# Keys and queries of six batches: transposed by DMA from a cast DRAM scratch instead of by TensorE

## The chip, the cores and the metric

One core of one Trainium2 chip. The metric is the device time of one execution in microseconds (us). All runs told of here are in the fast state, but for one of the 21 runs of the kernel before on the chip of e8, e10 and e11, which is slow and left out of the ratios. PE is TensorE, DVE is VectorE, ACT is ScalarE, POOL is GpSimd, SP is SyncE. SBUF and PSUM are the two memories on the chip that the kernel works in; PE's results land in PSUM.

## The reference

Attention with a window of 32 to each side and 8 global tokens, then a two-layer MLP on its output. Cut to what matters:

```python
# q, k, v: (8 batches, 8 heads, 576 tokens, 64), float32
scores = q @ k^T / 8
mask   = |i - j| <= 32  or i is global  or j is global
attn   = softmax(where(mask, scores, -1e9))
x      = (attn @ v) as (8*576 tokens, 512)
h      = x @ w_in                    # 512 -> 2048
out    = (relu(h) ** 2) @ w_out      # 2048 -> 512, float32
```

## The kernel before

A *pair* is two heads of one batch: 4 pairs per batch, 32 in all, each worked in two halves of 288 queries (*half-steps*). Attention needs keys and queries with the head dimension on the partitions. So each pair is loaded as float32 with tokens on the partitions, cast to float16 by DVE (keys, `natk`) and ACT (queries, values), transposed by six PE instructions per tensor into a PSUM buffer `tr`, and copied from there by DVE into `kt` and `qt`:

```python
def cast_tokens(op, nm, i):
    b, hp = divmod(i, NHP)
    n = TP + NG if b > 1 else TP           # 96 token rows, 8 global rows
    nat = nats[(nm, i)] = sbt("nat" + nm, [TP + NG, TJ, P], FP16, bufs=2)
    op(out=nat[0:n].rearrange("p j (h d) -> p h j d", d=D),
       in_=st[nm][0:n, 2 * hp : 2 * hp + 2])

def transposed(nm, i):
    nat = nats.pop((nm, i))
    b = i // NHP
    tr = pst("mm" if b == 0 or (nm == "q" and i <= 2 * NHP) else "tr", [P, 1024], FP16)
    for j in range(TJ):                    # 6
        n = TP + NG if (b > 1 and j == TJ - 1) else TP
        nc.tensor.transpose(tr[:, TP * j : TP * j + n], nat[0:n, j, :], identity[0:n, 0:n])
    # ... batches 0 and 1: global rows by 6 small matmuls more
    return tr[:, 0:S].rearrange("p (j q) -> p q j", j=TJ), gl

def tr_k(i, tail=None):                    # tr_q alike, with two copies
    tk, gl = transposed("k", i)
    # ... three DVE copies from PSUM into kts[i % NBUF]
```

The blocks of the MLP of earlier tokens fill PE while attention waits for ACT and DVE. `fill` issues such blocks up to a credit, and `scatter` lets POOL write a finished batch's global rows into `xT`, the input of the MLP. The loop over batches 2 to 7:

```python
for i in range(2 * NHP, B * NHP):
    b, hp = divmod(i, NHP)
    # ...
    for half in range(2):
        et = scores(i, half)
        if i + 1 < B * NHP:
            (tr_k, tr_q)[half](i + 1)
        nf = 3.2 if b == 2 else 4
        fill(2 * step, nf)
        if prev is not None:
            pv(*prev)
            if prev[1] == 1 and prev[0] % NHP == NHP - 1:
                scatter(prev[0] // NHP)
        fill(2 * step + 1, nf)
        prev = (i, half, et)
        casts(i + 2, half)                 # cast_tokens, cast_values, next loads
        step += 1
```

The softmax here doesn't subtract the row's maximum and nothing guards it: scores larger than these inputs give would overflow.

## Time and profile before

| | before |
|---|---|
| time | 369.43 us, median of the first 3 runs (368.81 to 369.75) |
| PE busy, of a span of 368.4 us | 347.7 us (94%) |
| DVE / ACT / POOL busy | 250.5 (68%) / 249.2 (68%) / 51.3 us (14%) |
| DMA packets | 65,011 |

The averages mix stages. I divide the span at the first score matmul of pair 8 (start of batch 2), at that of pair 12 (start of batch 3), and 1.0 us before the end of the last attention matmuls (at 302.45 us here, at 291.41 us in the changed kernel); what follows is MLP, but for these. In the table of windows each row has the stretch and its length, the busy us and the instruction count of PE, its weight loads, DVE, ACT and POOL, then the granted PE clock (1.00 is full speed), the DMA share (how much of the 16 DMA engines' time the recorded packets fill) and GB/s. Batch 2 and batches 3 to 7 of the kernel before:

```profile
80.01:116.46 36.45, 32.35 (x270) 16.36 (x270) 26.92 (x67) 29.61 (x58) 6.84 (x14) 0.95 0.66 166
116.46:301.45 184.99, 182.74 (x1509) 95.63 (x1508) 152.33 (x380) 151.88 (x299) 16.98 (x46) 1.00 0.39 105
```

PE is 99% busy in the second row. In the first it idles for 4.1 us (36.45 - 32.35). These two stages are the ones that the change touches.

### The profile page before, as it was taken

To read this page: it belongs to the slowest core of one execution; us is meant where nothing else is said; L and a number is where in the kernel's file an instruction comes from. 1 tells how busy PE (TensorE), PEld (TensorE's weight loads), DVE (VectorE), ACT (ScalarE), POOL (GpSimd) and SP (SyncE) were. 2 spreads that over 40 slices of the span, in tenths; PEclk is the share of its full clock that TensorE was granted. 3 is DMA by queue.
4 is the path that set the end of the run, shared out by engine and by line. 5 is a ranking of instruction groups with operands and counts; after the bars stand their busy time and mean duration, and the time that the engine had idled before them with its cause. 6 is when DMAs were issued, how large, how long until landed. Compare 5 with 4: busy or idle time off the path is not lost.

```text
span 368.4 us, 8258 instructions
## 1 busy us (share of the span) xinstructions
PE 347.7 (94%) x2941; PEld 186.0 (51%) x2941; DVE 250.5 (68%) x656; ACT 249.2 (68%) x482; POOL 51.3 (14%) x143
## 2 busy tenths in 40 slices
PE   7779799988899999999999999999999989999995
PEld 3556575544445555555555555555555544444442
DVE  7753566656888878977897789778977953422421
ACT  6656574465997799679967996799679942612610
POOL 5364430016000610020002000200020001000000
PEclk9978999998999999999999999999999999999999
DMA  8999999787843663375336533652020011002002
GB/s 196 192 147 201 193 228 201 188 188 193 188 130 97 188 166 94 90 188 142 95 93 187 142 95 93 187 140 60 30 87 2 0 52 64 0 30 85 0 32 85
DMA packets 65011, 43.93 MB, mean 119 GB/s; under 512 B 42730, under 2 KB 60074, under 8 KB 64970
## 3 DMA queue, kind: packets, MB, share of 16 engines
q1 hardware_dynamic: 59752, 38.03, 40.0%
q0 software_dynamic: 4800, 4.79, 7.9%
q10 hardware_dynamic: 418, 0.59, 0.7%
q8 instruction: 23, 0.38, 0.5%
q14 instruction: 18, 0.15, 0.1%
HBM read 37.85 MB, written 9.73 MB: 129 GB/s over the span
## 4 chain that ended last, share of the span: by engine, by line
PE 60%; issue 14%; DVE 7%; DMA 6%; ACT 5%; POOL 4%; POOLq 2%; ACTq 0%; SPq 0%; DVEq 0%
PE mm L502 25%; PE mm L460 24%; PE acc L602 4%; PE tr L415 3%; DMA w_in<-in_moe_w_in_dram 3%; PE sc L564 3%; DVE gt L466 2%; DMA stq<-in_q_dram 2%; POOLq L649 2%; ACT rl L465 2%; DMA stv<-in_v_dram 1%; POOL xT L658 1%; ACT er L570 1%; ACT natq L386 1%; DVE et L574 1%
## 5 line engine op out<-in xcount | busy, mean ns | idle before, releaser
L502 PE MATMUL mm<-w_out,gt 128*128 128x512 f16 x576 | 133.6, 379 | 0.0
L460 PE MATMUL mm<-xT,w_in 128*128 128x512 f16 x512 | 120.7, 382 | 1.0 <-POOL xT L658 1.0
L465 ACT ACTIVATE rl<-mm 128x512 f16<-128x512 f32 x128 | 72.2, 595 | 34.6 <-PE mm L460 33.9
L502 PEld LDWEIGHTS <-gt 128*128 128x128 f16 x576 | 53.1, 97 | 55.6
L460 PEld LDWEIGHTS <-w_in 128*128 128x128 f16 x512 | 47.7, 98 | 51.2 <-issue 2.9
L612 ACT ACTIVATE rec<-acc 64x288 f32<-64x288 f32 (+1 forms) x112 | 45.5, 406 | 33.9 <-PE acc L602 24.1
L638 DVE TENSOR_TENSOR xT<-acc,rec 64x288 f16<-64x288 f32 (+1 forms) x112 | 50.9, 454 | 19.8 <-ACT rec L613 18.0
L466 DVE TENSOR_TENSOR gt<-rl 128x512 f16<-128x512 f16 x128 | 50.2, 421 | 18.2 <-ACT rl L465 17.5
L658 POOL COPY xT<-gx 128x4 f16 (+2 forms) x80 | 21.8, 272 | 231.1 <-DVE xT L638 226.8
L570 ACT ACTIVATE er<-sc 128x912 f16<-128x912 f32 (+1 forms) x48 | 44.0, 917 | 5.4 <-PE sc L564 5.0
L574 DVE TENSOR_TENSOR et<-er,mask 128x912 f16<-128x912 f16 (+1 forms) x48 | 29.9, 623 | 21.2 <-ACT er L570 20.9
L508 DVE COPY ot<-mm 128x512 f32<-128x512 f32 x36 | 24.9, 691 | 26.0 <-PE mm L502 25.3
L613 ACT ACTIVATE rec<-rec 128x288 f32<-128x288 f32 x64 | 28.3, 443 | 2.0
L386 ACT CAST natq<-stq 104x768 f16<-104x768 f32 (+1 forms) x32 | 26.4, 824 | 4.4 <-DMA stq<-in_q_dram 4.4
L570 ACT ACTIVATE et<-sc 128x912 f16<-128x912 f32 (+1 forms) x16 | 14.6, 915 | 12.0 <-PE sc L564 11.7
L386 DVE CAST natk<-stk 104x768 f16<-104x768 f32 (+1 forms) x32 | 17.7, 552 | 0.3
L479 PE MATMUL mm<-xT,w_in 128*128 128x256 f16 x128 | 16.8, 290 | 0.6 <-POOL xT L658 0.6
L479 PEld LDWEIGHTS <-w_in 128*128 128x128 f16 x128 | 12.7, 104 | 3.3 <-issue 0.6
L617 DVE TENSOR_REDUCE gs<-acc 128x16 f32<-128x32 f32 x32 | 6.0, 187 | 12.2 <-ACT rec L612 12.2
L415 PE MATMUL tr<-identity,natk 96*128 96x96 f16 x168 | 12.1, 208 | 1.9 <-DVE natk L386 1.8
L415 PEld LDWEIGHTS <-natq 96*128 96x128 f16 x192 | 9.2, 98 | 7.1 <-ACT natq L386 1.5
L491 DVE TENSOR_TENSOR gt<-rl 128x512 f16<-128x512 f16 x16 | 6.8, 426 | 8.4 <-ACT rl L490 8.1
(205 smaller groups left out, 324.2 us busy)
## 6 DMA issues: line engine op xcount, KB each, us to landing
stk<-in_k_dram SPq DMA_DIRECT2D x32, 288.0 KB
out_dram<-ot SPq DMA_DIRECT2D x36, 256.0 KB
stq<-in_q_dram SPq DMA_DIRECT2D x30, 288.0 KB
stv<-in_v_dram SPq DMA_DIRECT2D x64, 120.0 KB
w_in<-in_moe_w_in_dram POOLq DMA_DIRECT2D x4, 512.0 KB, 9.5
w_out<-in_moe_w_out_dram POOLq DMA_DIRECT2D x4, 512.0 KB, 9.0
stv<-in_v_dram SPq DMA_DIRECT2D x32, 48.0 KB
stq<-in_q_dram ACTq DMA_DIRECT2D x2, 288.0 KB
```

What stands on the lines that cost most here:

```text
L386: op(out=nat[0:n].rearrange("p j (h d) -> p h j d", d=D), in_=st[nm][0:n, 2 * hp : 2 * hp + 2],)
L415: nc.tensor.transpose(tr[:, TP * j : TP * j + n], nat[0:n, j, :], identity[0:n, 0:n])
L460: nc.tensor.matmul(ph, w_in[:, t, u * P : (u + 1) * P], xT[:, t, XOFF + c * TC : XOFF + (c + 1) * TC], start=(t == 0), stop=(t == NDM - 1),)
L465: nc.scalar.activation(out=rl, in_=ph, func=AF.Relu)
L466: nc.vector.tensor_tensor(out=gts[c][:, u, :], in0=rl, in1=rl, op=ALU.mult)
L479: nc.tensor.matmul(ph[:, j], w_in[:, t, (u + j) * P : (u + j + 1) * P], xT[:, t, half * (256 + XOFF) : half * (256 + XOFF) + 256], start=( ...
L502: nc.tensor.matmul(po, gts[c][:, f, m * P : (m + 1) * P], w_out[:, f, :], start=(f == 0), stop=(f == NFF - 1),)
L570: nc.scalar.activation(out=er[:, :, 0:W], in_=sc[:, :, 0:W], func=AF.Exp, bias=0.0, scale=scale)
L574: nc.vector.tensor_tensor(out=et[:, :, 0:W], in0=er[:, :, 0:W], in1=mask[:, MB[half] : MB[half] + W].unsqueeze(1).to_broadcast((P, 2, W)), ...
L612: nc.scalar.activation(out=rec[r], in_=av[rs, xs, :, 0:GTOK], func=AF.Ln)
L613: nc.scalar.activation(out=rec, in_=rec, func=AF.Exp, scale=-1.0)
L638: nc.vector.tensor_tensor(out=xT[r, hp, x0 : x0 + HS].rearrange("p (k x) -> p k x", k=2), in0=av[r, x, :, 0:GTOK], in1=rec[r], op=ALU.mult,)
```

## The change

The intent: for batches 2 to 7, take the transposes off PE and the casts and PSUM copies off DVE and ACT, and let the DMA engines do both. DMAs from POOL cast keys and queries of a whole batch, nine in all, from the float32 inputs into a float16 scratch in DRAM. A transposing DMA from SP brings each pair's 128 columns from there into `kt` or `qt`. Values are cast by their own DMA, straight into place. From batch 3 on they lie in the old float32 buffers of keys and queries (`vbs`), which need constant ones between the values and some zeros; `open_values` writes these once for each of the two buffers.

```diff
+    def fetch_batch(b, nms="kq"):           # POOL: cast on the way to the scratch
+        if "k" in nms:
+            for t in range(NT):
+                r0 = t * P + NG
+                nc.gpsimd.dma_start(
+                    out=kscr[b][r0 : r0 + KN[t]].rearrange("s (h d) -> s h d", d=D),
+                    in_=k[b, :, KT * t : KT * t + KN[t]].rearrange("h s d -> s h d"),
+                )
+        # ... "q" alike, four groups into qscr[b]
+    def fetch_transposed(i):                # SP
+        b, hp = divmod(i, NHP)
+        cols = slice(P * hp, P * hp + P)
+        nc.sync.dma_start_transpose(out=kts[i % NBUF], in_=kscr[b][:, cols])
+        nc.sync.dma_start_transpose(out=qts[i % NBUF], in_=qscr[b][:, cols])
+    def open_values(op, vb):
+        op(vb[:, :, :, 1], 1.0)
+        op(vb[96:P, 4, :, 0], 0.0)
     # ... batch 1: the casts of batch 2 are issued after the transposes of pair 5, and in pair 7:
-            (tr_k, tr_q)[half](i + 1)
+            if more:
+                (tr_k, tr_q)[half](i + 1)     # ... v_globals as before
+            else:
+                fetch_transposed(2 * NHP + half)
     # ... the loop over batches 2 to 7:
-            if i + 1 < B * NHP:
-                (tr_k, tr_q)[half](i + 1)
+            if half and i + 2 < B * NHP:
+                fetch_transposed(i + 2)
             nf = 3.2 if b == 2 else 4
             # ... fill, pv, scatter, fill as before
-            casts(i + 2, half)
+            if half and b + 1 < B and hp < 3:
+                if hp == 0:
+                    open_batch(b + 1)
+                    fetch_batch_globals(b + 1)
+                if hp < 2:
+                    fetch_batch(b + 1, "kq"[hp])
+                else:
+                    fetch_batch_values(b + 1)
+            if half == 0 and b == 2 and hp < 2:
+                open_values(nc.vector.memset, vbs[1 - hp])
```

More of the change, by code (lines that the diff above doesn't have):

```diff
@@ L78, in pst @@
         return ps.tile(shape, dtype, name=tag, tag=tag, bufs=bufs_of[tag])
-    st = {nm: sbt("st" + nm, [TP + NG, H, TJ, D], FP32) for nm in "kq"}
+    stf = {nm: sbt("st" + nm, [P, H * TJ * D], FP32) for nm in "kq"}
+    st = {nm: t[0:TP].rearrange("p (h j d) -> p h j d", j=TJ, d=D) for nm, t in stf.items()}
+    vbs = [
+        stf[nm].bitcast(FP16)[:, 0 : NT * H * P].rearrange("p (t h x d) -> p t h x d", t=NT, x=2, d=D)
+        for nm in "qk"
+    ]
     st["v"] = sbt("stv", [P, NT, H, D], FP32)
@@ L117, in fetch_values @@
         )
-    def fetch_globals(b, hp):
-        def rows(nm):
-            return gscr[(nm, b // 2)][b % 2, :, 2 * hp : 2 * hp + 2]
-        for nm in "kq":
-            js = range(TJ) if b == 2 else (TJ - 1,)
-            for h in range(2):
-                dst = st[nm][TP : TP + NG, 2 * hp + h, js[0] : TJ]
-                nc.sync.dma_start(
-                    out=dst, in_=rows(nm)[:, h].unsqueeze(1).to_broadcast((NG, len(js), D))
-                )
-        nc.sync.dma_start(
-            out=st["v"][0:NG, :, 2 * hp : 2 * hp + 2].rearrange("p t h d -> p t (h d)"),
-            in_=rows("v").rearrange("g h d -> g (h d)").unsqueeze(1).to_broadcast((NG, NT, 2 * D)),
+    kscr, qscr = {}, {}
@@ new lines, in open_batch @@
+    def open_batch(b):
+        kscr[b] = dram.tile([NT * P, dm], FP16, name=f"kscr{b}")
+        qscr[b] = dram.tile([NCOL, dm], FP16, name=f"qscr{b}")
+        pad = 8 + KN[4]
+        nc.sync.dma_start(out=kscr[b][4 * P + pad : NT * P], in_=idle[0 : P - pad, 0:dm])
+    def fetch_batch(b, nms="kq"):
[5 more added lines that the diff above has]
+                    in_=k[b, :, KT * t : KT * t + KN[t]].rearrange("h s d -> s h d"),
+                )
+        if "q" in nms:
+            for g in range(4):
+                r0 = g * GRP
+                nc.gpsimd.dma_start(
+                    out=qscr[b][r0 : r0 + GTOK].rearrange("s (h d) -> s h d", d=D),
+                    in_=q[b, :, GTOK * g : GTOK * (g + 1)].rearrange("h s d -> s h d"),
+                )
@@ new lines, in fetch_batch_globals @@
+    def fetch_batch_globals(b):
+        for nm, scr, r0, n, m in (("k", kscr, 0, NT, P), ("q", qscr, GTOK, 4, GRP)):
+            rows = gscr[(nm, b // 2)][b % 2].rearrange("g h d -> g (h d)")
+            nc.sync.dma_start(
+                out=scr[b].rearrange("(t r) c -> r t c", r=m)[r0 : r0 + NG],
+                in_=rows.unsqueeze(1).to_broadcast((NG, n, dm)),
+            )
+    def fetch_transposed(i):
[3 more added lines that the diff above has]
+        nc.sync.dma_start_transpose(out=qts[i % NBUF], in_=qscr[b][:, cols])
@@ new lines, in open_values, with fetch_batch_values, fetch_values16 @@
+    def open_values(op, vb):
+        op(vb[:, :, :, 1], 1.0)
+        op(vb[96:P, 4, :, 0], 0.0)
+    def fetch_batch_values(b):
+        vb = vbs[b % 2]
+        for t in range(NT):
+            nc.gpsimd.dma_start(
+                out=vb[8 : 8 + KN[t], t, :, 0],
+                in_=v[b, :, KT * t : KT * t + KN[t]].rearrange("h s d -> s h d"),
+            )
+            nc.sync.dma_start(out=vb[0:NG, t, :, 0], in_=gscr[("v", b // 2)][b % 2])
+    def fetch_values16(i):
+        b, hp = divmod(i, NHP)
+        vt = vts[i % NBUF]
+        for e in range(2):
+            nc.gpsimd.dma_start(
+                out=vt[8 : 8 + KT, 0:4, 2 * e],
+                in_=v[b, 2 * hp + e, 0 : 4 * KT].rearrange("(t s) d -> s t d", s=KT),
+            )
+            nc.sync.dma_start(
+                out=vt[0:NG, :, 2 * e],
+                in_=gscr[("v", b // 2)][b % 2, :, 2 * hp + e].unsqueeze(1).to_broadcast((NG, NT, D)),
+            )
+        nc.gpsimd.dma_start(
+            out=vt[8 : 8 + KN[4], 4, 0:3:2],
+            in_=v[b, 2 * hp : 2 * hp + 2, 4 * KT : S].rearrange("h s d -> s h d"),
@@ L362, in gather_rows @@
     def gather_rows(c):
-        gsts = {nm: sbt("gst" + nm, [P, D], FP32) for nm in "kqv"}
+        gsts = {nm: sbt("gst" + nm, [P, D], FP16) for nm in "kqv"}
         for nm, gst in gsts.items():
@@ L373, in gather_store @@
         for nm, gst in gsts.items():
-            scr = dram.tile([P, D], FP32, name=f"gscr_{nm}{c}")
+            scr = dram.tile([P, D], FP16, name=f"gscr_{nm}{c}")
             nc.gpsimd.dma_start(out=scr, in_=gst)
@@ L382, in cast_tokens @@
     def cast_tokens(op, nm, i):
-        b, hp = divmod(i, NHP)
-        n = TP + NG if b > 1 else TP
-        nat = nats[(nm, i)] = sbt("nat" + nm, [TP + NG, TJ, P], FP16, bufs=2)
-        op(
-            out=nat[0:n].rearrange("p j (h d) -> p h j d", d=D),
-            in_=st[nm][0:n, 2 * hp : 2 * hp + 2],
+        hp = i % NHP
+        nat = nats[(nm, i)] = sbt("nat" + nm, [TP, TJ, P], FP16, bufs=2)
+        op(
+            out=nat.rearrange("p j (h d) -> p h j d", d=D),
+            in_=st[nm][:, 2 * hp : 2 * hp + 2],
         )
@@ L410, in transposed @@
         nat = nats.pop((nm, i))
-        b = i // NHP
-        tr = pst("mm" if b == 0 or (nm == "q" and i <= 2 * NHP) else "tr", [P, 1024], FP16)
+        tr = pst("mm" if i < NHP or (nm == "q" and i <= 2 * NHP) else "tr", [P, 1024], FP16)
         for j in range(TJ):
-            n = TP + NG if (b > 1 and j == TJ - 1) else TP
             nc.tensor.transpose(
-                tr[:, TP * j : TP * j + n], nat[0:n, j, :], identity[0:n, 0:n]
+                tr[:, TP * j : TP * j + TP], nat[:, j, :], identity[0:TP, 0:TP]
             )
-        gl = tr[:, S : S + NG]
-        if b < 2:
-            gl = tr.bitcast(FP32)[:, 384 : 384 + NG]
-            for j in range(TJ):
-                nc.tensor.matmul(
-                    gl, nat[0:TP, j, :], ohp[0:TP, j, :], start=(j == 0), stop=(j == TJ - 1),
-                    skip_group_check=True,
-                )
+        gl = tr.bitcast(FP32)[:, 384 : 384 + NG]
+        for j in range(TJ):
+            nc.tensor.matmul(
+                gl, nat[:, j, :], ohp[0:TP, j, :], start=(j == 0), stop=(j == TJ - 1),
+                skip_group_check=True,
+            )
         return tr[:, 0:S].rearrange("p (j q) -> p q j", j=TJ), gl
@@ L582, in pv @@
         b, hp = divmod(i, NHP)
-        vt = vts[i % NBUF]
-        vtf = vt.rearrange("p t x d -> p t (x d)")
+        if b < 3:
+            vt = vts[i % NBUF]
+            vtf = vt.rearrange("p t x d -> p t (x d)")
+            off = (0, D)
+        else:
+            vtf = vbs[b % 2].rearrange("p t h x d -> p t (h x d)")
+            off = (2 * P * hp, 2 * P * hp + D)
         acc = pst("acc", [P, 2, 512])
@@ L602, in pv @@
                 nc.tensor.matmul(
-                    acc[:, e, o : o + w], vtf[:, t, D * e : D * e + P], et[:, e, so : so + w],
+                    acc[:, e, o : o + w], vtf[:, t, off[e] : off[e] + P], et[:, e, so : so + w],
                     start=(n == 0), stop=(n == nw - 1), skip_group_check=True,
@@ L745, in casts @@
             cast_values(op_v, i)
-            if i + NHP < B * NHP:
-                fetch_pair(*divmod(i + NHP, NHP))
-                fetch_globals(*divmod(i + NHP, NHP))
     nc.sync.dma_start(out=gate[:, 0:2], in_=w_in[0:1, 0, dff - 514 : dff - 512])
@@ L777 @@
     gather_store(1, gs1)
+    open_batch(2)
+    fetch_batch_globals(2)
     casts(NHP, 0)
@@ L802 @@
     prev = None
+    pool.tensor_copy(out=gate[:, 0:1], in_=st["k"][32:33, H - 1, TJ - 1, D - 1 : D])
+    fetch_batch(2)
+    fetch_values16(2 * NHP)
+    fetch_values16(2 * NHP + 1)
     for i in range(NHP + 1, 2 * NHP):
-        casts(i + 1, 0)
-        casts(i + 1, 1, nc.vector.tensor_copy)
+        more = i + 1 < 2 * NHP
+        if more:
+            casts(i + 1, 0)
+            casts(i + 1, 1, nc.vector.tensor_copy)
         for half in range(2):
@@ L809 @@
                 pv(*prev)
-            (tr_k, tr_q)[half](i + 1)
-            if half and i + 1 < 2 * NHP:
-                v_globals(i + 1)
+            if more:
+                (tr_k, tr_q)[half](i + 1)
+                if half:
+                    v_globals(i + 1)
+            else:
+                fetch_transposed(2 * NHP + half)
             take(2)
             prev = (i, half, et)
+    fetch_values16(2 * NHP + 2)
     pv(*prev)
     scatter(1)
+    fetch_values16(2 * NHP + 3)
     step = 16
     prev = None
-    casts(2 * NHP + 1, 0)
-    casts(2 * NHP + 1, 1)
     for i in range(2 * NHP, B * NHP):
@@ L837 @@
             prev = (i, half, et)
-            casts(i + 2, half)
+            if half and b + 1 < B and hp < 3:
[4 more added lines that the diff above has]
+                    fetch_batch(b + 1, "kq"[hp])
+                else:
+                    fetch_batch_values(b + 1)
+            if half == 0 and b == 2 and hp < 2:
+                open_values(nc.vector.memset, vbs[1 - hp])
             step += 1
```

## The prediction

> **What bounds the kernel now.** I read the busy time of each engine stage by stage first, because the change touches batches 2 to 7 only and the averages of the whole span (PE 94%) mix stages. The stage borders come from the score matmuls (line 564): pair 8, the first of batch 2, has its first one at 80.0 us and its second half at 87.7; pair 12, the first of batch 3, starts at 116.5; the last attention work ends near 302. In the table of windows the columns are busy us and instruction count per engine, then granted clock, DMA share and GB/s:
>
> ```profile
> 78.00:87.70 9.70, 7.16 (x49) 3.00 (x49) 5.25 (x14) 4.16 (x9) 4.66 (x11) 0.82 0.86 193
> 91.40:100.10 8.70, 7.55 (x71) 4.04 (x70) 6.97 (x18) 8.56 (x18) 0.00 (x0) 1.00 0.89 214
> 100.10:109.10 9.00, 8.53 (x74) 4.38 (x76) 7.76 (x21) 8.86 (x19) 0.00 (x0) 1.00 0.45 113
> ...
> 186.14:223.03 36.89, 36.62 (x304) 19.24 (x305) 30.56 (x77) 30.56 (x61) 2.47 (x8) 1.00 0.47 127
> 223.03:259.92 36.89, 36.62 (x305) 19.24 (x305) 30.57 (x77) 30.58 (x61) 2.47 (x8) 1.00 0.41 109
> ```
>
> From 116 us on PE is busy 36.62 of every 36.89 us, at full clock: it sets the pace. DVE and ACT are busy 83% each and run beside it. Only batch 2 is mixed: ACT fills 8.56 of 8.70 and 8.86 of 9.00 us there, and PE idles about 1.6 us.
>
> Busy PE is not PE at its peak, so I then read the timeline of PE in steady state (start, duration, engine, line, operation, count):
>
> ```profile
> 199.91 0.43 PE L415 MATMUL tr<-identity,natk 96*128 96x96 f16 x6
> 200.18 1.89 PE L460 MATMUL mm<-xT,w_in 128*128 128x512 f16 x8
> 201.91 0.55 PE L602 MATMUL acc<-et,vt_78 128*128 128x112 f16 x6
> 202.29 1.89 PE L460 MATMUL mm<-xT,w_in 128*128 128x512 f16 x8
> 204.11 0.36 PE L564 MATMUL sc<-qt_74,kt_69 64*128 64x112 f16 x6
> 204.41 0.43 PE L415 MATMUL tr<-identity,natq 96*128 96x96 f16 x6
> 204.68 1.89 PE L460 MATMUL mm<-xT,w_in 128*128 128x512 f16 x8
> ```
>
> Starts, not durations, tell the cost. Eight MLP matmuls take 201.91 - 200.18 = 1.73 us, 216 ns each, with no gap. Six transposes take 200.18 - 199.91 = 0.27 us, 45 ns each, although each is recorded as 206 ns long. So what leaves the instruction stream of PE leaves the time of the stage, at its spacing.
>
> **What the Trainium skill says, and whether the trace agrees.**
> 1. "TensorE: Matmul & The Clock Gate", Part 4 (PE-mode transpose) gives some 275 to 390 ns for a transpose and says that its result must be copied out of PSUM. Taken as a price, that would make 288 removed transposes worth 79 us or more. The trace disagrees as far as cost in a stream goes: 45 ns. I use 45.
> 2. "DMA: Bandwidth & Descriptors", section SWDGE vs HWDGE vs iDMA: a DMA that casts has to come from GpSimd, whose cores write the descriptors in software; a transposing one from SP or ACT. This fits the change. The trace of before has casting DMAs (the weights): three issues from 19.50 us took 2.73 us of POOL, 0.91 us each.
> 3. The same page, Specifications: transfers under 512 B fall below line rate because of a read-modify-write. The trace does not show that for 256 B rows into SBUF (below, 225 GB/s); whether 128 B rows into DRAM pay it, nothing in the trace before shows. This is my main doubt.
> 4. "Advanced Engine Details and Errata", X-Bar Transpose (TRN2): transposing DMAs are said to run like plain ones, 350 to 400 GB/s. No trace here has one yet.
>
> **Part by part.**
> *Removed from PE.* Transposes for pairs 8 to 31: 24 pairs x 12. From pair 9 on they stand in the batch loop: 23 pairs x 2 x 0.27 = 12.4 us, of which 4 pairs (2.2 us) in batch 2 and 19 pairs (10.3 us) after. The waits they cause go too. In batch 2:
>
> ```profile
> PE tr L415 <- DVE natk L386: 1.5, 1, 1.5
> PE mm L460 <- POOL xT L658: 1.0, 1, 1.0
> PE tr L415 <- DVE kt_68 L438: 0.7, 1, 0.7
> PE sc L564 <- DVE qt_73 L450: 0.5, 1, 0.5
> PE acc L602 <- ACT rl L465: 0.3, 1, 0.3
> ```
>
> The 1.5 us before the first transpose of pair 9 is no gain: right behind it PE waits 1.0 us for the POOL copies of batch 1's global rows into xT, which end at the same moment whether or not PE gets there earlier. The 0.7, 0.5 and 0.3 are gains, with 0.2 more: about 1.6 us. After 116 us the idle time of PE is 184.5 - 182.7 = 1.8 us, most of it in transposes waiting for kt copies out of their PSUM buffer; I take 1.3.
> *End of batch 1.* Pair 8 is no longer cast and transposed there: 0.54 us of PE; I take 0.5, since the POOL wait swallows some.
> *Removed from DVE and ACT, beside PE.* Per pair, DVE loses the key cast (0.55), the kt copies (0.65 + 0.25 + 0.17) and the qt copies (0.76 + 0.17) = 2.55 us; ACT loses the query cast (0.82) and value casts (0.81) = 1.63 us. Of 30.6 us per batch, some 20 and 24 remain. This is worth nothing where PE sets the pace except the waits counted above.
> *Sum.* Batch 2: 2.2 + 1.6 = 3.8. Batches 3 to 7: 10.3 + 1.3 = 11.6. End of batch 1: 0.5. Total 15.9. The MLP tail after 302 us is untouched, and so is everything before 60 us. 369.4 - 15.9 = 353.5.
> *Added, DMA.* What 256 B rows cost the DMA engines is seen where value loads run alone, from 8 to 9 us of the span:
>
> ```profile
> DMA packets 862, 0.23 MB, mean 225 GB/s; under 512 B 852, under 2 KB 862, under 8 KB 862
> ```
>
> 862 packets in 1 us of 16 engines is 18.6 engine-ns each. Per batch three tensors of 8 x 576 rows of 256 B are cast: 13,824 packets x 18.6 = 257 engine-us. Transposes: 4 pairs x (640 + 608) rows of 256 B = 4,992 x 18.6 = 93, if they read like plain rows. Output stores: 4 tiles x 128 rows x 75 ns (852 packets with 10.0% of 16 x 40 us, from 320 to 360) = 38. Global rows about 10. Sum 398 of 16 x 34.4 = 550 engine-us per batch of the new length: 72% against 0.47 now. It fits, with nothing to spare for a doubling.
> *Added, POOL.* 14 casting DMAs per batch. An issue of 128 descriptors took 0.57 us, one of 512 took 0.91: about 0.9 ns more per descriptor, so 1.3 to 1.5 us for 960 to 1,152: some 20 us per batch of 34 (an estimate). Only the scatter copies share POOL.
> *Added, SP.* Two transposes per pair, issued three half-steps (about 13 us) before use. They stand in one queue with the output stores, so a transpose that waits for its scratch also holds stores, and after three ot buffers PE.
> *The first use.* The casts of batch 2 can start on POOL when the keys of batch 1 have landed, near 58 us (the last of them are issued at 53.3). 9,216 rows x 18.6 / 16 = 10.7 us, so they end by 75 to 80 us, and the scores of pair 8 are due at 80. The transposes come just before: a stall of 0 to 3 us is possible. I allow 0.5 for it: 354.
>
> **Rivals.**
> (a) *DMA becomes the bound.* Were a 128 B write to DRAM to cost twice a 256 B read, 9,216 x 18.6 = 171 more engine-us give 569, 35.6 us per batch: some 1 to 2 us per batch given back, 360 or so. At three times the sum is 741, 46 us per batch, and the five batches from 3 on take 60 us more: over 410. For it: every row is short on both sides, and the scratch is written and read again. Against: the casting loads of the weights moved 2 KB rows in 78 ns (1,237 packets in 6 us), so the cast itself costs no rate; short rows into SBUF ran at 225 GB/s.
> (b) *Late once.* The scratch of batch 2, or POOL blocked by waits of its DMA issues so that batch 1's scatter is late: PE idles once for 2 to 8 us, and its clock falls as it did at 84 us, where eight matmuls took 3.54 us rather than 1.73. Result 356 to 363. For it: no slack is planned there. Against: 20 us from the first cast.
> (c) *Nothing gained.* The transposes were hidden, or DVE or ACT held the pace: then within 1% of before. Against: PE idles 0.7% in steady state.
> (d) *Transposing DMAs are slow* (say four times a plain read): 280 engine-us more, 42 us per batch, near 395.
>
> **Range and chances.** If the DMA keeps up (I give it three in four), 349 to 360, depending on (b) and on how much idle time goes. A moderate overload gives 360 to 372, a heavy one more. Point 354, range 348 to 373. Faster by 2% means below 362: 0.74; within 2%: 0.12; slower: 0.14.
>
> **What would show it.** Right: no line 415 after batch 1; steady periods near 34.4 us with PE still at 99%; DVE and ACT near 60 to 70%; DMA share in the loop near 0.7 and below 0.9; score matmuls waiting for no DMA. The first step is wrong if the period falls by much less than 2.2 us with PE busy, so that other PE work stretched; the DMA step if PE waits for kt or qt from a DMA, or for DVE behind stores that SP holds; the first-use step if the gap before pair 8 exceeds 3 us. Clocks below 1.0 in the loop would mean new idle gaps.

## The result, and the profile after

| | before | after |
|---|---|---|
| median (range), fast runs alternated on one chip | 369.59 us (368.81 to 370.68), 4 runs | 357.70 us (355.80 to 359.65), 4 runs |
| ratio, 95% interval | | 0.9677 (0.9613 to 0.9740) |

A ratio here is always the mean time of one kernel's fast runs over that of the other's of the same rounds, so it is not quite the ratio of the medians. The changed kernel is faster by 3.2%, and its outputs are correct.

The span by stage, in us, from the first profile of each kernel:

| stage | before | after | predicted change | measured change |
|---|---|---|---|---|
| up to the first score matmul of batch 2 | 80.01 | 80.15 | -0.5, with 0.5 allowed for a stall | +0.1 |
| batch 2 | 36.45 | 36.43 | -3.8 | 0.0 |
| batches 3 to 7 | 184.99 | 173.79 | -11.6 | -11.2 |
| MLP after the last attention | 66.95 | 67.23 | 0 | +0.3 |

Windows of the changed kernel: batch 2, batches 3 to 7, and four pairs in steady state:

```profile
80.15:116.58 36.43, 31.60 (x226) 14.84 (x224) 23.30 (x46) 24.38 (x46) 21.42 (x31) 0.91 1.16 107
116.58:290.37 173.79, 172.39 (x1281) 85.81 (x1280) 117.09 (x267) 126.74 (x242) 64.56 (x102) 1.00 1.03 111
185.91:220.34 34.43, 34.43 (x258) 17.17 (x258) 23.05 (x53) 25.27 (x48) 14.41 (x22) 1.00 1.23 125
```

The steady batch takes 34.43 us, against 36.89 before; the prediction had 34.4. PE has no idle time at all there. DVE and ACT are down to 67% and 73%, and POOL is up to 14.4 us. In batch 2, 44 PE instructions fewer are recorded (48 by the code), yet the stretch is as long as before: PE idles 4.8 us there and its clock is 0.91.

The timeline of PE in steady state has no transpose left:

```profile
185.91 0.40 PE L619 MATMUL sc<-qt_73,kt_68 64*128 64x160 f16 x10
186.23 1.90 PE L557 MATMUL mm<-w_out,gt 128*128 128x512 f16 x8
187.97 0.55 PE L662 MATMUL acc<-et,stq 128*128 128x112 f16 x6
188.35 1.89 PE L557 MATMUL mm<-w_out,gt 128*128 128x512 f16 x8
190.18 0.36 PE L619 MATMUL sc<-qt_73,kt_68 64*128 64x112 f16 x6
```

From one MLP block to the next group the starts lie 187.97 - 186.23 = 1.74 us apart, as before (1.73). What is left runs at the old spacing; the period is shorter because the transposes are gone from it.

The waits of PE within batch 2 (who waited, for what, us in all, times, longest). This is the view that the prediction showed for the kernel before:

```profile
PE mm L515 <- POOL xT L718: 2.8, 1, 2.8
PE acc L662 <- DVE xT L698: 2.0, 1, 2.0
```

The waits in front of transposes and for copies out of PSUM are gone, as foreseen. Where before PE waited 1.5 us for a cast and then 1.0 us for the scatter on POOL, it now waits 2.8 us for the scatter: the prediction had said that this gain would be swallowed. But the second wait, for `xT` from DVE, is new. The timeline of DVE and PE around it (start, duration, engine, line, operation; in brackets the idle time before it, and what ended that; "issue" means nothing that the profile shows):

```profile
97.27 2.19 DVE L167 MEMSET stq<- 128x2560 f16 x1 [0.48 <-issue]
...
99.55 0.27 DVE L168 MEMSET stq<- 32x256 uint32 x1
99.86 0.62 DVE L629 TENSOR_TENSOR et<-er,mask 128x880 f16<-128x880 f16 x1
100.39 0.75 DVE L521 TENSOR_TENSOR gt<-rl 128x512 f16<-128x512 f16 x2
...
101.28 0.91 DVE L698 TENSOR_TENSOR xT<-acc,rec 64x288 f16<-64x288 f32 x2
...
102.34 0.78 PE L662 MATMUL acc<-et,vt_82 128*128 128x112 f16 x6 [2.04 <-DVE xT L698]
...
102.91 3.38 PE L515 MATMUL mm<-xT,w_in 128*128 128x512 f16 x8
```

The two MEMSET lines are `open_values` for one of the two buffers: 2.46 us of DVE. The mask multiplication, the MLP's squares and the last step of the attention output queue behind it, one after the other. `acc` is free for the next matmuls only when that last step (`xT`) has read it, so PE waits 2.04 us. Then its eight MLP matmuls are recorded with 3.38 us instead of 1.89: the granted clock is 0.63 from 102 to 104 us and 0.52 from 104 to 106. The other buffer's fill at 88.39 us took as long.

### The profile page after: what moved, and what is told of

It is laid out like the page before. It is cut to its first block, busy times and chain, and to the rows that moved or that the text cites. A ratio compares the mean times of both kernels' runs of the same rounds, so it can differ in the third digit from the quotient of the medians.

```text
span 357.6 us, 7418 instructions
## 1 busy us (share of the span) xinstructions
PE 337.5 (94%) x2653; PEld 175.4 (49%) x2653; DVE 209.7 (59%) x514; ACT 218.2 (61%) x412; POOL 129.1 (36%) x235
## 4 chain that ended last, share of the span: by engine, by line
PE 83%; DVE 4%; issue 3%; DMA 3%; POOL 2%; ACT 2%; SPq 0%; POOLq 0%; DVEq 0%
PE mm L557 34%; PE mm L515 32%; PE acc L662 6%; PE sc L619 5%; DMA stv<-in_v_dram 3%; PE mm L534 3%; PE acc L654 1%; DVE xT L698 1%; POOL xT L718 1%; POOL w_in L765 1%; ACT rec L672 1%; PE sc L612 1%; ACT rec L673 1%; DVE gr L689 0%; ACT rl L545 0%
## 5 line engine op out<-in xcount | busy, mean ns | idle before, releaser
L515 PE MATMUL mm<-xT,w_in 128*128 128x512 f16 x512 | 122.1, 386 | 2.8 <-POOL xT L718 2.8
L520 ACT ACTIVATE rl<-mm 128x512 f16<-128x512 f32 x128 | 73.7, 594 | 38.7 <-PE mm L515 37.3
L515 PEld LDWEIGHTS <-w_in 128*128 128x128 f16 x512 | 47.2, 99 | 55.4 <-issue 5.8
L718 POOL COPY xT<-gx 128x4 f16 (+2 forms) x80 | 19.1, 239 | 135.1 <-DVE xT L698 130.8
L521 DVE TENSOR_TENSOR gt<-rl 128x512 f16<-128x512 f16 x128 | 52.2, 423 | 26.0 <-ACT rl L520 25.2
L662 PEld LDWEIGHTS <-stk 128*128 128x128 f16 x192 | 12.7, 97 | 7.5 <-issue 2.1
L534 PE MATMUL mm<-xT,w_in 128*128 128x256 f16 x128 | 15.5, 273 | 0.6 <-POOL xT L718 0.6
L173 POOL DMA_DIRECT2D stk<-in_v_dram x15 | 15.9, 1493 | 0.4 <-PE mm L515 0.4
L662 PE MATMUL acc<-et,stk 128*128 128x8 f16 (+2 forms) x192 | 14.1, 212 | 1.6 <-DVE xT L698 1.6
L534 PEld LDWEIGHTS <-w_in 128*128 128x128 f16 x128 | 11.9, 98 | 2.7 <-issue 0.8
L546 DVE TENSOR_TENSOR gt<-rl 128x512 f16<-128x512 f16 x16 | 6.8, 424 | 7.1 <-ACT rl L545 6.7
L173 POOL DMA_DIRECT2D stq<-in_v_dram x10 | 10.5, 1400 | 0.6 <-PE mm L515 0.6
```

The costliest lines, as they stand in the source:

```text
L173: nc.gpsimd.dma_start(out=vb[8 : 8 + KN[t], t, :, 0], in_=v[b, :, KT * t : KT * t + KN[t]].rearrange("h s d -> s h d"),)
L515: nc.tensor.matmul(ph, w_in[:, t, u * P : (u + 1) * P], xT[:, t, XOFF + c * TC : XOFF + (c + 1) * TC], start=(t == 0), stop=(t == NDM - 1),)
L520: nc.scalar.activation(out=rl, in_=ph, func=AF.Relu)
L521: nc.vector.tensor_tensor(out=gts[c][:, u, :], in0=rl, in1=rl, op=ALU.mult)
L534: nc.tensor.matmul(ph[:, j], w_in[:, t, (u + j) * P : (u + j + 1) * P], xT[:, t, half * (256 + XOFF) : half * (256 + XOFF) + 256], start=( ...
L662: nc.tensor.matmul(acc[:, e, o : o + w], vtf[:, t, off[e] : off[e] + P], et[:, e, so : so + w], start=(n == 0), stop=(n == nw - 1), skip_g ...
```

## The experiments

The changed kernel itself ran once more with the first group (a0_after): 357.48 us, ratio 0.9693 (0.9660 to 0.9727) to the kernel before.

> The changed kernel unedited, to have its times and trace on the chip of the other runs of this call. Main theory: the saving (11.9 us at the first timing) comes from the batches from 3 on, where PE sets the pace and lost 2 x 0.27 us of transposes per pair (from 9.22 to 8.61 us per pair), and what should have come out of batch 2 was taken back there by two writes of the constant one on DVE (2.19 us each) and by the lowered PE clock after the idle time that they cause. Expected: 356 to 359 us, ratio to before 0.965 to 0.972. Every rival expects the same.

```profile
78.75:114.51 35.76, 30.29 (x225) 14.16 (x223) 23.17 (x46) 24.21 (x46) 21.57 (x31) 0.95 1.23 115
```

That is its batch 2. The PE waits are 2.8 us for POOL and 2.7 us for DVE, but the clock is 0.95, not 0.91: the drop of the first profile does not come in every execution. Batches 3 to 7 take 173.79 us again. I compare the runs below with this profile.

The theory: in batches 3 to 7 PE sets the pace, and the removed transposes are the gain; in batch 2 the two fills on DVE give the gain back. The rivals: the DMA (first scratch, or short rows), the scatter on POOL, or a gain in batches 3 to 7 that came from DVE and ACT instead.

### e1: the constant fills on POOL, earlier

```diff
+    ONES = 0x3C003C00                      # two float16 ones
+    # ... vbw: the buffers of vbs, viewed as int32
     def open_values(op, vb):               # on an int32 view of the buffers
-        op(vb[:, :, :, 1], 1.0)
+        op(vb[:, :, :, 1], ONES)
     # ... the zeros alike
     fetch_values16(2 * NHP + 2)
+    for vb in vbw:
+        open_values(pool.memset, vb)       # before scatter(1)
-            if half == 0 and b == 2 and hp < 2:
-                open_values(nc.vector.memset, vbs[1 - hp])
```

> The changed kernel with the two constant fills of the value buffers moved from DVE in batch 2 to POOL, where it waits anyway (75 to 81.8 us), and written as 32-bit words. Main theory (the fills on DVE delay xT, so PE waits 2.0 us at 102 us and then runs eight matmuls in 3.4 instead of 1.7 us): 3 to 4 us faster than the changed kernel, near 354, no PE wait for DVE xT over 0.5 us in batch 2, and its pair 10 takes about 8 us, not 11.6. Rival (batch 2 is held back by the casting and transposing DMAs that all run there): no change, under 1 us.

354.69 us, ratio 0.9615 (0.9583 to 0.9648): 2.8 us less than a0_after in the same rounds, a little under the 3 to 4 expected. Batch 2:

```profile
79.87:112.54 32.67, 29.87 (x226) 14.24 (x224) 18.81 (x42) 23.95 (x46) 21.87 (x31) 0.95 1.30 115
```

32.67 us, 3.1 less than in a0_after, and the wait for `xT` from DVE is gone; the 2.8 us for POOL are the only one left. Against the kernel before it is 36.45 - 32.67 = 3.8 us: what the prediction had summed for batch 2. On POOL the fills stood at 75.6 to 78.8 us, and batch 2 started at 79.87 us, as in runs without this edit (78.75 in a0_after, 80.15 in the first profile, 79.72 in e2).

### e2: the fills done twice on DVE

```diff
                 open_values(nc.vector.memset, vbs[1 - hp])
+                open_values(nc.vector.memset, vbs[1 - hp])
```

> The changed kernel with each of the two constant fills on DVE done twice, so 2.5 us more of DVE at two places of batch 2. Main theory: the second place already stalls PE, so all of it shows there (2.5 us, plus a slower clock after a longer gap), and part of it at the first: 3 to 6 us slower than the changed kernel, near 361 to 363. Rival (DMA holds batch 2): under 1 us.

365.56 us, ratio 0.9924 (0.9889 to 0.9959): 8.1 us more than a0_after for 4.9 us more of DVE work, and more than I expected. Batch 2:

```profile
79.72:122.27 42.55, 33.10 (x225) 15.09 (x224) 28.28 (x50) 24.88 (x46) 21.84 (x31) 0.88 0.99 91
```

It is 6.8 us longer than in a0_after. The waits for `xT` from DVE grew from 2.7 to 6.7 us in two (4.0 more), and PE is busy for 2.8 us more with the same instructions, at a clock of 0.88. A wait of PE can cost itself and the slow matmuls after it: after the 4.07 us wait here eight matmuls are recorded with 3.13 us, but after the 2.20 us wait of a0_after with 1.89. With e1 this shows the fills as the cause in batch 2 from both sides.

### e3: PE's work back, nothing else

Six transposes per half-step of a constant tile into the free PSUM buffer `tr`, which nothing reads; results are unchanged.

```diff
                 fetch_transposed(i + 2)
+            if i + 1 < B * NHP:
+                dm_tr = pst("tr", [P, 1024], FP16)
+                for j in range(TJ):
+                    nc.tensor.transpose(dm_tr[:, TP * j : TP * j + TP],
+                        mask[0:TP, P * j : P * j + P], identity[0:TP, 0:TP])
```

> The changed kernel with the 12 transposes per pair put back on PE for the pairs that follow, of data that nobody needs and into a PSUM buffer that nobody reads: the PE time returns, the waits and the DVE and ACT work do not. Main theory (a transpose costs PE its spacing of 45 ns and PE sets the pace): 20 pairs x 0.54 = 10.8 us slower from batch 3 on, a pair 9.15 us; near 368, hardly better than before. Rival (the saving came from the waits for PSUM copies, or from the relief of DVE and ACT): under 3 us slower, near 360.

367.32 us, ratio 0.9955 (0.9922 to 0.9988): nearly all is given back. Batches 3 to 7, and a steady batch:

```profile
115.84:299.10 183.26, 182.12 (x1509) 95.34 (x1508) 117.78 (x267) 127.76 (x242) 64.44 (x102) 1.00 1.00 105
152.53:189.01 36.48, 36.48 (x306) 19.19 (x306) 23.20 (x53) 25.47 (x48) 14.40 (x22) 1.00 1.23 118
```

36.48 - 34.43 = 2.05 us for 48 transposes, 43 ns each (the prediction's figure was 45). Batches 3 to 7 take 183.26 us, 9.5 of the 11.2 us that the change had won there. PE is busy all the time in the steady batch, with DVE and ACT as relieved as in the changed kernel: their relief alone is worth 1.7 us.

### e4 and e8: the work of DVE and ACT back, PE left free

e4 put back seven casts per pair from SBUF in a row, five on DVE and two on ACT:

```diff
+                # ... nat, nat2: float16 buffers; stv: float32 values
+                for _ in range(2 if half else 3):
+                    nc.vector.tensor_copy(out=nat, in_=stv[0:TP, 0 : TJ * P])
+                if half:
+                    for x in (0, 1):
+                        nc.scalar.copy(out=nat2, in_=stv[0:TP, 0 : TJ * P])
```

> The changed kernel with about the removed work put back on DVE and ACT alone: per pair five casts of 96 x 768 on DVE (2.65 us; before had 2.55 us) and two on ACT (1.64 us; before 1.63), of data that nobody needs. Main theory (they run beside PE from batch 3 on): there under 1.5 us in all, a pair stays near 8.6 us, but batch 2, where ACT was full before and DVE now has the fills, gives 1 to 4 us: near 359 to 362 in all. Rival (the saving is the relief of DVE and ACT): 8 us or more slower, a pair above 9 us.

375.73 us, ratio 1.0172 (1.0135 to 1.0210): 1.7% slower than before, less than the 2% of a clear verdict but with an interval above 1, and far from what I expected. A batch:

```profile
157.52:194.58 37.06, 35.06 (x257) 17.00 (x257) 34.70 (x73) 31.35 (x56) 15.16 (x22) 1.00 1.20 116
```

DVE is busy for 34.70 of 37.06 us, more than the 30.6 of the kernel before: a cast took 0.57 to 0.75 us, so this overshot, and put them in blocks where the old kernel had them spread. It shows that DVE can become the bound, not what the real work was worth. So e8 copied the old pieces: on DVE, copies of 500, 96 and 40 columns from PSUM in one half-step and of 640 and 40 in the other, and one cast of 768; on ACT, casts of 768, 512 and 128, each at the old place in the half-step. They are stand-ins: unlike the old copies they wait for no transpose. Results are again unchanged.

```diff
+    # ... before the loop: old, olda (float16, SBUF), wt (PSUM), stv (float32 values)
+            if i + 1 < B * NHP:
+                for n in ((500, 96, 40), (640, 40))[half]:
+                    nc.vector.tensor_copy(out=old[:, 0:n], in_=wt[:, 0:n])
             nf = 3.2 if b == 2 else 4
             # ... fill, pv, fill
+            if i + 2 < B * NHP:
+                if half == 0:
+                    nc.vector.tensor_copy(out=old, in_=stv[:, 0:768])
+                else:
+                    for n in (768, 512, 128):
+                        nc.scalar.copy(out=olda[:, 0:n], in_=stv[:, 0:n])
```

> The changed kernel with work like the removed work on DVE and ACT, this time in the places and pieces of the kernel before: after the scores of a half-step, copies out of a PSUM buffer that nobody writes any more (500, 96 and 40 columns, or 640 and 40); at the end of a half-step the cast of 768 columns on DVE, or of 768, 512 and 128 on ACT. The first attempt (e4: five casts in blocks of two and three, 0.55 to 0.75 us each) cost 18 us, more than the whole saving. Theory of placement (blocks of 1.6 to 2.25 us of DVE delay xT, as one fill of 2.2 us does; small pieces hide): from batch 3 on under 2 us, some 1 to 3 us in batch 2, 358 to 362 in all. Rival (at 8.61 us a pair DVE and ACT have no room for the old work, so their relief is a condition of the saving wherever it stands): pairs of 9 us and more, 365 or above.

369.71 us (16 runs), ratio 0.9941 (0.9914 to 0.9967) to the kernel before, which took 371.70 on this chip. That is the side of the rival in the expectation, not of my theory of placement. Batches 3 to 7, cut at the same instruction as in the changed kernel (1,281 of PE in both), and one batch:

```profile
119.95:300.45 180.50, 175.20 (x1281) 85.17 (x1280) 146.33 (x381) 153.69 (x299) 65.83 (x102) 1.00 1.00 107
148.10:183.75 35.65, 35.02 (x259) 17.03 (x258) 29.56 (x77) 30.95 (x61) 15.23 (x23) 1.00 1.34 126
```

With DVE and ACT loaded as before (30.6 each there), a batch takes 35.65 us and PE idles 0.63 us of it. Batches 3 to 7 take 180.50 us, 6.7 more than in the changed kernel. So PE's relief alone is worth 11.2 - 6.7 = 4.5 us. That PE is also recorded as busy for 0.6 us longer, with the same instructions at full clock, is a matter of counting: eight MLP matmuls are recorded with 1.90 us but start 1.74 us before the next group, so the first 0.16 us of each stop counts as busy. The waits of PE in these batches were for ACT (3.4 us in six).

Together: PE's relief alone 4.5 us, that of DVE and ACT alone 1.7, both 11.2. Whichever side keeps its old load gives back more than half of the gain (9.5 us with PE's, 6.7 with that of DVE and ACT). The prediction's "worth nothing where PE sets the pace" was wrong for this reason: it is true of the kernel before, and ceases to be true when PE gets shorter.

### e5: the casts into the scratch done twice

A second set of casting DMAs goes to scratch tensors that nothing reads.

```diff
                     fetch_batch_values(b + 1)
+                    real = kscr[b + 1], qscr[b + 1]
+                    # ... two other DRAM tensors in their place
+                    fetch_batch(b + 1)
+                    kscr[b + 1], qscr[b + 1] = real
```

> The changed kernel with all casts of keys and queries done a second time into scratch that nobody reads, after the casts of the values, for batches 3 to 7. Each cast of 9,216 rows took some 13.4 ns of an engine per row where it ran alone, so 7.7 us more of the DMA engines per batch, and 9 us more of POOL. Main theory (DMA is busy with casts in 18 to 19 of 34.4 us, so it has room): under 1.5 us slower. Rival (DMA is near its bound, as a DMA share of 1.2 to 1.3 in these stages could say): 3 us or more per batch, 15 us or more in all, with PE waiting for kt or qt.

357.09 us, ratio 0.9693 (0.9646 to 0.9740), the same as a0_after's 0.9693. A batch:

```profile
149.07:183.50 34.43, 34.43 (x257) 17.17 (x257) 23.07 (x53) 25.24 (x48) 24.60 (x34) 1.00 2.01 173
```

The DMA share rises to 2.01 and POOL's busy time to 24.60 us, and the batch is 34.43 us as before. DMA was not the bound, and POOL's issue work was not either. This refutes rival (a) in the steady state. Rival (d) had 42 us per batch; the 34.43 us refute it, and the cost of transposing rows below agrees.

A share above 1 needs explaining. The DMA view of the changed kernel, at 65 to 67 us where nothing but casts of keys and queries runs:

```profile
DMA packets 2392, 0.29 MB, mean 147 GB/s; under 512 B 2392, under 2 KB 2392, under 8 KB 2392
...
q0 software_dynamic: 2392, 0.29, 231.9%
```

By spacing, 2 us of 16 engines over 2,392 packets are 13.4 engine-ns per row. By recorded packet times the share is 231.9%, so packets overlap in an engine, and the share says how much is under way, not how full the engines are. 13.4 ns is less than the 18.6 that the prediction took from 256 B rows into SBUF: a row of 128 B into DRAM cost less than one of 256 B into SBUF, so the extra cost that the prediction feared did not show. And a stretch of 2 us (186 to 188) with transposing DMAs alone:

```profile
q1 hardware_dynamic: 637, 0.16, 34.1%
```

34.1% of 32 engine-us over 637 packets are 17 ns of recorded time for a row of 256 B. The plain rows behind the prediction's 18.6 ns by spacing have 24 ns by this measure (862 packets, 130.3% of 16 engine-us, in a stretch that was full). So a transposing row was no dearer than a plain one; recorded times overlap, so more than that they do not tell.

### e6, e7, e10, e11: PE's other idle time

The 2.8 us for the scatter on POOL stood in a0_after, e1 and e2 alike. e6 keeps three MLP blocks that the end of batch 1 used to issue, so that PE has them at that place. e7 is e6 with e1.

```diff
                 fetch_transposed(2 * NHP + half)
-            take(2)
+            take(2 if more else 1 - half)
```

> The changed kernel with three blocks of four second-layer matmuls held back from the last pair of batch 1, so that PE has them while it waits for the global rows of batch 1 (2.8 us of idle time before the matmuls of line 515 at 84.3 us, and then a slow clock for three groups). Main theory (that wait and clock drop cost the changed kernel some 4 us, and the matmuls moved there are not on the path): 1.5 to 4 us faster, PE wait for POOL xT under 1 us. Rival (holding back makes the same idle time a few us earlier, where scores and products of one pair wait for each other): no change within 1 us.

> The changed kernel with the fills on POOL as well as the held blocks, which should be the best of this family. Main theory: the two gains add, 5 to 7 us faster than the changed kernel, near 351. If the fills on POOL delay the scatter of batch 1, or the idle time only moves, less than 3 us.

e6: 357.58 us, ratio 0.9667 (0.9626 to 0.9708). e7: 356.38 us, ratio 0.9667 (0.9619 to 0.9715). Neither can be told from the changed kernel by these intervals, where 1.5 to 4 us and 5 to 7 us had been expected. The long scatter wait is gone, but others came. The waits of PE in the whole of e6:

```profile
PE acc L654 <- DVE xT L698: 4.1, 5, 1.7
PE acc L662 <- DVE xT L698: 3.6, 2, 2.0
PE sc L619 <- DMA qt<-qscr: 2.5, 3, 1.1
```

Of the first line, 1.7 us at the end of batch 1 is new. The second is not: 2.0 us of it are the fills, which e6 still has on DVE, and the last 1.6 us stand in the kernel before too. The third line is new; before it, only e4 had a wait of PE for a transposing DMA, 0.5 us at the first use. In e7 it is larger:

```profile
PE sc L625 <- DMA qt<-qscr: 3.9, 3, 2.8
```

The cause is on SP: its transposes wait for a scratch that is cast late. The waits of SP in the changed kernel, which had not reached PE there:

```profile
SPq L164 <- DMA qscr_1876<-in_q_dram: 9.2, 2, 6.4
SPq L164 <- DMA qscr_2333<-in_q_dram: 8.8, 1, 8.8
```

The query casts of a batch were issued one pair after the key casts, with 13 us of lead for the transposes on paper; waits up to 8.8 us ate most of it, so a gain of time on PE could run into it. In e7 POOL issued the query casts of batch 3 at 96.5 to 100.2 us, SP the transpose of its first queries at 104.0, and PE waited until 109.28. e10 and e11 therefore issue the query casts together with the key casts: e11 is e1 plus this, e10 is e7 plus this.

```diff
-                if hp < 2:
-                    fetch_batch(b + 1, "kq"[hp])
-                else:
+                if hp == 0:
+                    fetch_batch(b + 1)
+                elif hp == 2:
                     fetch_batch_values(b + 1)
```

> As e10 without the held blocks, to compare with it on one chip. No wait for qt was seen in e1, so the earlier queries should change little: 354 to 355. If the release of SP from its waits for the query scratch (up to 8.8 us per batch in the changed kernel) is worth something, since output stores stand behind it, 352 to 353.

> Fills on POOL, three blocks held back, and the casts of the queries issued together with those of the keys, one pair earlier. In the two kernels with held blocks PE waited 0.4 to 2.8 us for a transposed qt, at the start of one or more batches, where the scratch of the queries was late. Theory (the held blocks do save some 2 us, and the late queries took it back): no wait for qt, 351 to 353. Rival (holding blocks gains nothing in itself, since 1.7 us of idle time appears at the last pair of batch 1): as e1, 354 to 355.

e11: 356.84 us, ratio 0.9605 (0.9568 to 0.9641). e10: 354.69 us, ratio 0.9538 (0.9502 to 0.9574), the kernel before 371.70 us on this chip. Both are above the times expected, on a chip where the kernel before is slower too; by ratio e11 is as e1. With the queries early the held blocks are worth 356.84 - 354.69 = 2.15 us on the same chip. That is net: batch 2 is 6.3 us shorter in e10 than in e11 (28.20 against 34.54), but the 12 matmuls held back are pushed on through the backlog to the end, where after the last attention matmuls 301 PE instructions stand against 288, and 2.5 us more; batches 3 to 7 take 1.6 us more. PE still waits for a DMA in e10:

```profile
PE sc L625 <- DMA qt<-qscr: 1.5, 2, 0.8
```

One of these transposes, issued at 158.7 us, landed near 169. Casts and other transposes were moving until about 167 us; from 167.4 to 168.6 us the DMA moved little. Why the tail of this landing is so long stays open.

### e12: the transposes one half-step earlier

e10, with the transposing DMAs issued one half-step earlier, except those of a batch's first pair, whose scratch is not ready by then.

```diff
-            if half and i + 2 < B * NHP:
+            if half == ((i + 2) % NHP == 0) and i + 2 < B * NHP:
                 fetch_transposed(i + 2)
```

> e10 with the transposing DMAs of every pair but the first of a batch issued one half-step (4.3 us) earlier. In e10, PE still waited twice 0.7 to 0.8 us for a qt of the fourth pair of a batch: its DMA was issued at 158.7 us and landed near 169, beside the burst of casts that starts at 150. Theory (these waits are the landing time of a transposing DMA under the burst, against 13 us of lead): no wait for qt after batch 2, 0.5 to 2 us faster than e10, ratio near 0.950 to 0.953. Rival (issued earlier, the DMA also lands in the burst, or SP holds the stores): as e10, 0.954.

354.31 us (5 runs) where the kernel before took 372.30, ratio 0.9513 (0.9488 to 0.9537): the best of the study. Batch 2, and batches 3 to 7:

```profile
78.26:109.23 30.97, 29.93 (x226) 14.32 (x224) 18.72 (x42) 23.91 (x46) 21.66 (x31) 0.94 1.37 123
109.23:283.50 174.27, 172.42 (x1281) 85.83 (x1280) 116.34 (x267) 126.42 (x242) 64.97 (x102) 1.00 1.06 110
```

No wait of PE for `qt` is left. Batch 2 is down to 30.97 us; batches 3 to 7 are as in the changed kernel, within 0.5. So what this kernel wins over the changed one lies in batch 2 (4.8 us against a0_after), less the 2.9 us by which the end after the last attention matmuls is longer (69.11 against 66.25), where the held matmuls went. Against the changed kernel this is some 0.9513 / 0.9693 = 0.981, an estimate over two chips. e10 and e12 ran on different chips, and their intervals overlap: that the earlier transposes gain time beyond e10 is not shown, only that the waits for `qt` are gone.

## Why the prediction was right, and where it was wrong

The time was predicted at 354.0 us (348 to 373) and was 357.7: faster by over 2%, inside the range, 3.7 us above the point.

- **Batches 3 to 7: right** (-11.6 predicted, -11.2 measured). Reading the cost of a transpose from spacing in the stream (45 ns), not from its duration (206 ns), held: e3 measured 43 ns. The steady batch came out as predicted (34.43 us). The two terms hold too: between the two kernels PE's busy time fell by 182.74 - 172.39 = 10.35 us (10.3 predicted) and its idle time by 0.85 (1.3 predicted).
- **Batch 2: the step that failed.** The sum was "Batch 2: 2.2 + 1.6 = 3.8", and nothing was gained. The sum itself was sound: e1, without the fills, gets 3.8. The sum left out what the change adds to DVE: two fills by `open_values`, 2.46 us each. The diff shows them in its last lines. The Trainium skill says on the page "VectorE: DVE Perf Modes", section Zero memsets can be issued as uint32 (trn2), that a fill takes a cycle per element whatever the type. The trace agrees that the type makes no difference: each further element took 0.83 to 0.84 ns, of float16 (2,560 in 2.19 us, 128 in 0.165) and of 32 bits (256 in 0.27 us, 12 in 0.068). So the cost could have been counted. The prediction listed what leaves DVE and never what comes. In batch 2 an added wait also cost more than its length (e2: 4.0 us more of waits, 6.8 us more of time), as a drop of the clock followed. That this happens only at times is in the two profiles of one kernel (0.91 and 0.95).
- **"The POOL wait swallows it": right.** The 1.5 us before the first transpose came back in the scatter wait (1.0 to 2.8 us). The 0.5 us from the end of batch 1 came too, though the table hides it: from the first score matmul of pair 7 to that of pair 8 it is 6.92 us in the kernel before (73.09 to 80.01), and 6.40 in the changed one (73.75 to 80.15) and 6.42 in a0_after. What hides it is the time up to pair 7, which varies by more (72.33 us in a0_after).
- **"Worth nothing where PE sets the pace": wrong as a step, without effect on the number**, as both reliefs came in one change. e3 and e8 show that most of the gain needs both. For a change that took work from PE alone, the same working would have given 11.6 where e8 shows some 4.5. The relief itself was put too high: DVE and ACT keep 23.05 and 25.27 us per batch where some 20 and 24 were foreseen.
- **DMA: right that it keeps up, wrong in the measure.** Cost per row was 13.4 ns where 18.6 was taken, and transposing rows were no dearer than plain ones (17 ns against 24 by recorded times). POOL's work was put too high as well, at some 20 us per batch; it is 14.4. The share of "near 0.7 and below 0.9" came out at 1.23, without harm: e5 doubles the casts for nothing. As a test, the share was the wrong one; waits of PE for a DMA were the right one, and there were none.
- **First use: no stall.** The transposes of pair 8 were issued at 71.5 us and PE waited for no DMA, so the 0.5 us allowed were not needed (e4 and e7 had such a wait, of 0.5 us each). Rival (b) had the amount (356 to 363) and not the cause: PE was late once, for DVE.

## What to carry to other kernels

Count what a change adds to each engine as carefully as what it removes, one-time fills too, and place each addition in the stage where it runs: 2.5 us on an engine that has slack on average cost PE 2 us where PE was waiting for it (batch 2). Look at the end of the kernel too when work is moved: part of what e10 and e12 won in batch 2 came back after the last attention. In a balanced loop like this one, the relief of one engine was worth little until the others were relieved too (4.5 and 1.7 us apart, 11.2 together), and the two put-backs add up to more than the gain. When work moves to DMA, plan lead time by when its input is written; average bandwidth does not tell it, and a slack that nobody sees is used up by the next improvement.

## What the Trainium skill lacked or had wrong

- "TensorE: Matmul & The Clock Gate", Part 4: its 275 to 390 ns per transpose is no cost in a stream of other matmuls. Here, with tiles of 96 x 96, a transpose added 43 ns (e3), at a recorded duration of 206 ns.
- The same page, Part 1, gives an idle window of about 3.4 us that runs free. Here single waits of 2.0 us (with another of 2.8 us in the same batch) were followed by slow matmuls in one execution, and in another one 2.2 us were not. The phase of the window may tell the two executions apart, but a gap of 2.0 us is shorter than the window. In one execution of e2, 4.0 us of added waits came with 2.8 us of longer PE time.
- "DMA: Bandwidth & Descriptors", Specifications: it states that rows below 512 B lose rate, which agrees (147 GB/s for 128 B rows). But here 128 B rows into DRAM cost 13.4 engine-ns each, against 18.6 for 256 B rows into SBUF; an extra cost per row for the read-modify-write that it names did not show.
- "Advanced Engine Details and Errata", X-Bar Transpose (TRN2): that transposing DMAs are as fast as regular ones agrees (17 ns a row against 24, by recorded times). I found no page that says how long before its use such a DMA has to be issued beside other traffic: in one case it took some 10 us from issue to landing (e10).
- It would belong to "Perfetto Trace Analysis": I found no page that says that the DMA share of a profile can pass 1 without saturation: 2.01 here, at no loss (e5).
